# Moving eight PSUM copies of the kv sums from ScalarE to VectorE

## Chip, cores and metric

One core of one Trainium2 chip. The metric is device time in microseconds (us); lower is better. Engines are named as in the profile: PE is TensorE's matmuls, PEld its weight loads, DVE VectorE, ACT ScalarE, POOL GpSimd, SP the engine that issues most DMAs. "L614" is line 614 of the kernel.

## The reference, cut to what matters

```python
S, D, H, Dh = 2048, 1024, 32, 32
q, k, v = split(x @ wqkv)                      # 32 heads of 32
phi_q = [softmax(q w_phi), softmax(-q w_phi)]  # 64 features per head
phi_k = [softmax(k w_phi), softmax(-k w_phi)]
kv  = einsum("bhsf,bhsd->bhfd", phi_k, v)      # summed over the whole sequence
z   = einsum("bhsf->bhf", phi_k)
num = einsum("bhqf,bhfd->bhqd", phi_q, kv)
o   = num / (einsum("bhqf,bhf->bhq", phi_q, z) + 1e-6)
a   = o @ wo
b   = x, with a gated FFN added to the one row that a router picks
out = g * a + (1 - g) * b                      # g = sigmoid(x . gate_w), per row
```

The kv sums need every row of the sequence, so the kernel has two halves: the k side builds kv in PSUM, the memory in which the kernel puts the results of its matmuls, then kv is copied in bf16 to SBUF, from where the matmuls of the q side read it. The change is in the copy between the two halves.

## The kernel before

The program goes through a scheduler that orders each engine's instructions. The parts that matter, cuts marked with "...":

```python
psA = ...tile_pool(name="psA", bufs=2, space=PSUM)   # pq tiles: two buffers
psK = ...tile_pool(name="psK", bufs=1, space=PSUM)   # kvps, later num: ONE buffer
kvps = psK.tile([P, 3 * 512], F32, name="kvps", tag="kvn")

def kv_finish(ops, copy):                            # L606
    kvr = kvps[:, 0:16 * KSTR].rearrange("p (j half c) -> p j half c", half=2, c=KSTR)
    for op in ops:
        jh, half, hh_, sg = op // 8, op // 4 % 2, op // 2 % 2, op % 2
        ...
        copy(out=KV[jh][h4 * 32:h4 * 32 + 32, sg, :, h4 * 33:h4 * 33 + 33],     # L614
             in_=kvr[q * 32:q * 32 + 32, js, half, hh_ * 33:hh_ * 33 + 33])

def q_front(sb, j):
    pq = psA.tile([P, SB], F32, name="pq", tag="pA")
    for kb in range(KB):                             # 8 matmuls: "a pq group"
        nc.tensor.matmul(pq[:], ...)                                            # L627
    nc.scalar.activation(out=E[:, j, 0, :], in_=pq[:], func=ACTF.Exp)           # L629
    nc.scalar.activation(out=E[:, j, 1, :], in_=pq[:], func=ACTF.Exp, scale=-1.0)  # L630

def q_num(t, hf):
    num = psK.tile([P, 3 * 512], F32, name="num", tag="kvn")
    ... 8 matmuls num <- E, KV[hf]                                              # L648
    nc.vector.reciprocal(out=rS, in_=nb[:, :, 132:136])                         # L657 (rq)
    ... T <- num * rS on VectorE                                                # L662

    kv_finish(range(8), nc.vector.tensor_copy)       # into KV[0]
    kv_finish(range(8, 16), nc.scalar.copy)          # into KV[1]
    ...
    while i < n_front + NL + 2 or wq_:               # the q side
        ... q_num of step i - 7 ...
        if NPRE <= i < n_front:
            q_front(i // KB, i % KB)
        ... q_wo: 8 matmuls "po" (L705), result to HBM
```

A pq group needs one of two PSUM buffers, which the second exponential of an earlier group frees. The first num needs the one buffer that kvps holds until the last of the 16 copies; in the trace of the kernel before it is recorded as waiting 0.98 us for them. The whole kernel:

Of the kernel before, what the change touches and what calls it, by code (L numbers as in the profile page):

```python
# [167 lines left out]
def kernel(  # L168
# [4 lines left out]
    nc = tc.nc  # L173
# [433 lines left out]
# [4 lines that stand above are left out]
            js = slice(jh * 4, jh * 4 + 4)  # L611
            h4 = half * 2 + hh_
            q = hh_ * 2 + sg
            copy(out=KV[jh][h4 * 32:h4 * 32 + 32, sg, :, h4 * 33:h4 * 33 + 33],  # L614
                 in_=kvr[q * 32:q * 32 + 32, js, half, hh_ * 33:hh_ * 33 + 33])
# [167 lines left out]
            one_hot_sums()  # L783
    qp["eb"] = None
    kv_finish(range(8), nc.vector.tensor_copy)
    kv_finish(range(8, 16), nc.scalar.copy)
    kscope.close()
    qp["eb"] = main.enter_context(tc.tile_pool(name="eb", bufs=1))
    qp["qw"] = main.enter_context(tc.tile_pool(name="qw", bufs=2))
# [77 lines left out]
```

## Time and profile before

| kernel before | |
|---|---|
| device time, median of 3 (range) | 280.58 us (280.07 to 280.60) |
| span of the profiled run | 279.5 us (a fourth run, 281.24 us long) |
| TensorE busy | 271.8 us, 97% |
| VectorE / ScalarE / GpSimd busy | 67% / 44% / 50% |
| the 16 copies (L614) | 8 on VectorE, median 292 ns; 8 on ScalarE, median 264 ns |

A timeline line has start, length, engine, line, operation, output<-input, count, and in brackets how long the engine was idle before it and what released it. "Pitch" is the time from one start to the next in a row of like instructions; small_ps are small matmuls of the FFN row, which the scheduler puts between the others. A line of the windows table has the stretch, its length, the busy us (and instructions) of PE, PEld, DVE, ACT and POOL, then the granted TensorE clock, the DMA share and GB/s. The engine that matters is TensorE, so what counts is where it stops. The lines are in the prediction.

### The profile page before, as it was taken

To read this page: it belongs to the slowest core of one execution; us is meant where nothing else is said; L and a number is where in the kernel's file an instruction comes from. 1 tells how busy PE (TensorE), PEld (TensorE's weight loads), DVE (VectorE), ACT (ScalarE), POOL (GpSimd) and SP (SyncE) were. 2 spreads that over 40 slices of the span, in tenths; PEclk is the share of its full clock that TensorE was granted. 3 is DMA by queue.
4 is the path that set the end of the run, shared out by engine and by line. 5 is a ranking of instruction groups with operands and counts; after the bars stand their busy time and mean duration, and the time that the engine had idled before them with its cause. 6 is when DMAs were issued, how large, how long until landed. Compare 5 with 4: busy or idle time off the path is not lost.

```text
span 279.5 us, 5440 instructions
## 1 busy us (share of the span) xinstructions
PE 271.8 (97%) x2022; PEld 149.7 (54%) x2022; DVE 186.2 (67%) x386; ACT 121.9 (44%) x235; POOL 140.9 (50%) x152
## 2 busy tenths in 40 slices
PE   7999999999999999999999899999999999999994
PEld 3666667676544455455554354554555555555442
DVE  3020025566799898699993287888766677899862
ACT  3143332232455546454564657855445543323300
POOL 8000000000087989847862078999566555798310
PEclk9999999999999999999999999999999999999999
DMA  7899993854963788985705817843897244425631
GB/s 257 215 177 187 161 179 76 133 107 130 394 258 114 276 311 298 353 295 189 281 0 188 302 49 260 201 99 13 28 174 202 68 94 125 129 96 133 150 98 62
DMA packets 68767, 47.97 MB, mean 172 GB/s; under 512 B 51376, under 2 KB 56576, under 8 KB 68736
## 3 DMA queue, kind: packets, MB, share of 16 engines
q1 hardware_dynamic: 68240, 47.10, 63.4%
q10 hardware_dynamic: 464, 0.48, 0.5%
q8 instruction: 17, 0.28, 0.4%
q14 instruction: 14, 0.11, 0.1%
q0 software_dynamic: 32, 0.00, 0.0%
HBM read 31.00 MB, written 4.20 MB: 126 GB/s over the span
## 4 chain that ended last, share of the span: by engine, by line
PE 83%; DMA 7%; DVE 4%; issue 2%; ACT 2%; POOL 2%; DVEq 0%; POOLq 0%
PE po L705 20%; PE pq L627 19%; PE pv L536 17%; PE pk L578 11%; PE num L648 6%; DMA wch<-in_B_w_up_dram 3%; DMA mrow<-mi 3%; PE pW L313 2%; PE kvps L602 2%; DVE ssum L586 2%; PE facc L475 1%; PE pv L558 1%; DMA xs_t<-in_A_x_dram 1%; PE kvps L558 1%; PE small_ps L490 1%
## 5 line engine op out<-in xcount | busy, mean ns | idle before, releaser
L578 PE MATMUL pk<-wkf,xT 128*128 128x512 bf16 x256 | 60.4, 379 | 0.0
L627 PE MATMUL pq<-xT,wqf 128*128 128x512 bf16 x256 | 60.2, 379 | 0.0
L677 POOL TENSOR_TENSOR U<-T 128x512 f32<-128x512 f32 x32 | 41.5, 1298 | 34.2 <-DVE T L662 16.7
L705 PE MATMUL po<-wo_sb,oT 128*128 128x512 bf16 (+2 forms) x264 | 58.6, 373 | 0.0
L536 PE MATMUL pv<-wv_sb,xT 128*128 128x256 bf16 (+2 forms) x336 | 52.9, 307 | 0.0
L593 POOL TENSOR_TENSOR phi<-e,rs 128x1024 bf16<-128x1024 bf16 x24 | 45.8, 1912 | 4.0 <-DVE cnd L343 2.4
L586 DVE TENSOR_REDUCE ssum<-e 128x32 f32<-128x1024 bf16 x32 | 38.1, 1194 | 3.8 <-ACT e L582 3.3
L705 PEld LDWEIGHTS <-oT 128*128 128x128 bf16 x264 | 25.4, 98 | 27.8
L536 PEld LDWEIGHTS <-xT 128*128 128x128 bf16 x336 | 31.4, 97 | 14.7
L662 DVE TENSOR_TENSOR T<-num,rq 128x1024 f32<-128x1024 f32 x32 | 38.9, 1215 | 0.0
L543 ACT CAST v_all<-pv 128x384 bf16<-128x384 f32 (+1 forms) x45 | 20.1, 447 | 41.8 <-PE pv L536 36.0
L627 PEld LDWEIGHTS <-wqf 128*128 128x128 bf16 x256 | 23.8, 98 | 24.1 <-issue 0.6
L708 DVE SCALAR_TENSOR_TENSOR o_out<-po,gate,xg 128x512 bf16<-128x512 f32 (+2 forms) x33 | 23.9, 729 | 18.4 <-PE po L705 17.2
L578 PEld LDWEIGHTS <-xT 128*128 128x128 bf16 x256 | 23.0, 97 | 22.8
L678 POOL TENSOR_TENSOR o_sb<-U,rden 128x512 bf16<-128x512 f32 x32 | 33.6, 1049 | 2.5
L581 ACT ACTIVATE e<-pk 128x512 bf16<-128x512 f32 x32 | 19.1, 597 | 32.3 <-PE pk L578 21.9
L629 ACT ACTIVATE E<-pq 128x512 bf16<-128x512 f32 x32 | 19.0, 595 | 30.5 <-PE pq L627 30.2
L423 POOL COPY wch<-wT 1x1 bf16<-1x1 bf16 x3 | 0.4, 177 | 58.6 <-DMA wT<-in_A_wqkv_dram 58.6
L590 POOL TENSOR_TENSOR ksum<-ksum,ssum 128x32 f32<-128x32 f32 x32 | 13.0, 405 | 20.7 <-DVE ssum L586 15.3
L648 PEld LDWEIGHTS <-E 128*128 128x128 bf16 x256 | 16.4, 98 | 10.5 <-DVE T L662 5.2
L648 PE MATMUL num<-KV,E 128*128 128x136 bf16 x256 | 20.7, 223 | 1.0 <-ACT KV L614 1.0
L630 ACT ACTIVATE E<-pq 128x512 bf16<-128x512 f32 x32 | 18.9, 591 | 0.0
(140 smaller groups left out, 253.7 us busy)
## 6 DMA issues: line engine op xcount, KB each, us to landing
wchd<-in_B_w_down_dram SPq DMA_DIRECT2D x7, 1024.0 KB
wch<-in_B_w_up_dram SPq DMA_DIRECT2D x6, 1024.0 KB
wch<-in_B_w_gate_dram SPq DMA_DIRECT2D x4, 1024.0 KB
xin<-in_A_x_dram SPq DMA_DIRECT2D x16, 256.0 KB
out_dram<-o_out SPq DMA_DIRECT2D x30, 128.0 KB
wch<-in_B_w_gate_dram SPq DMA_DIRECT2D x4, 768.0 KB
wv_sb<-in_A_wqkv_dram SPq DMA_DIRECT2D x8, 256.0 KB
wo_sb<-in_A_wo_dram SPq DMA_DIRECT2D x1, 2048.0 KB
```

What stands on the lines that cost most here:

```text
L536: nc.tensor.matmul(pv[:, 0:hi - lo], lhsT=xT[:, kb, t * P:(t + 1) * P], rhs=wv_sb[:, kb, lo:hi], start=(kb == 0), stop=(kb == KB - 1))
L543: nc.scalar.copy(out=v_all[:, t, h0:h1, 0:DH], in_=pv[:, 0:(h1 - h0) * DH].rearrange("p (h d) -> p h d", d=DH))
L578: nc.tensor.matmul(pkf, lhsT=xT[:, kb, t * P:(t + 1) * P], rhs=wkf[:, kb, hf * 512:(hf + 1) * 512], start=(kb == 0), stop=(kb == KB - 1))
L586: nc.vector.tensor_reduce(out=ssum[:], in_=e2, axis=AX.X, op=ALU.add)
L593: eng.tensor_tensor(out=phi[:].rearrange("p h s f -> p (h s) f"), in0=e2, in1=_bc(rs[:], [P, HH * 2, DH]), op=ALU.mult)
L627: nc.tensor.matmul(pq[:], lhsT=wqf[:, kb, j * P:(j + 1) * P], rhs=xT[:, kb, sb * SB:(sb + 1) * SB], start=(kb == 0), stop=(kb == KB - 1))
L648: nc.tensor.matmul(num[:, b * NSTR:b * NSTR + KVW], lhsT=E[:, j, sg, tl * P:(tl + 1) * P], rhs=KV[hf][:, sg, jl, :], start=True, stop=True)
L662: nc.vector.tensor_tensor(out=T[:].rearrange("p s (j h) d -> p (s j) h d", h=4), in0=nv[:, :, :, 0:DH], in1=rS.unsqueeze(3).to_broadcast([ ...
L677: nc.gpsimd.tensor_tensor(out=U[:], in0=T[:, 0], in1=T[:, 1], op=ALU.add)
L678: nc.gpsimd.tensor_tensor(out=st["o"][:, hf * HH:(hf + 1) * HH, :], in0=U[:], in1=_bc(rden[:], [P, HH, DH]), op=ALU.mult)
L705: nc.tensor.matmul(po[:, 0:w], lhsT=st["oT"][:, kb, :], rhs=wo_sb[:, kb, sl], start=(kb == 0), stop=(kb == KB - 1))
L708: nc.vector.scalar_tensor_tensor(out=o_out[:, 0:w], in0=po[:, 0:w], scalar=gate[:, t:t + 1], in1=st["xg"][:, sl], op0=ALU.mult, op1=ALU.add)
```

## The change

Its intent: all copies of the kv sums on VectorE, which is idle there (4.88 us, from its own eight copies to rq); ScalarE is relieved.

```diff
     kv_finish(range(8), nc.vector.tensor_copy)
-    kv_finish(range(8, 16), nc.scalar.copy)
+    kv_finish(range(8, 16), nc.vector.tensor_copy)
     kscope.close()
```

## The prediction

> **What bounds the kernel now.** I read the page of the kernel before first: busy times, then the chain that ended last.
>
> ```profile
> span 279.5 us, 5440 instructions
> PE 271.8 (97%) x2022; PEld 149.7 (54%) x2022; DVE 186.2 (67%) x386; ACT 121.9 (44%) x235; POOL 140.9 (50%) x152
> PE 83%; DMA 7%; DVE 4%; issue 2%; ACT 2%; POOL 2%; DVEq 0%; POOLq 0%
> ```
>
> TensorE is busy 97% of the span and 83% of the chain is its work. The other engines matter only where TensorE stops for them. The change touches 16 small copies of the kv sums out of PSUM (line 614), so I asked next for the waits of that line's neighbourhood, 152.7 to 162.1 us (engine, line, what it waited for, us in total, times, longest):
>
> ```profile
> DVE rq L657 <- PE num L648: 4.9, 1, 4.9
> DVE KV L614 <- PE kvps L602: 2.9, 1, 2.9
> PE num L648 <- ACT KV L614: 1.0, 1, 1.0
> ACT KV L614 <- DVE KV L614: 0.2, 1, 0.2
> ```
>
> TensorE waits once, 1.0 us, for ScalarE's copies; ScalarE's copies wait for VectorE's, although they fill another tile; VectorE then has 4.9 us of nothing to do. The timeline of the same stretch (start, length, engine, line, operation, count) shows the order:
>
> ```profile
> 152.72 3.61 PE L627 MATMUL pq<-xT,wqf 128*128 128x512 bf16 x16
> 152.91 2.44 DVE L614 CAST KV<-kvps 32x132 bf16<-32x132 f32 x8 [2.93 <-PE kvps L602]
> 154.64 0.60 ACT L629 ACTIVATE E<-pq 128x512 bf16<-128x512 f32 x1 [1.15 <-PE pq L627]
> 155.39 2.19 ACT L614 CAST KV<-kvps 32x132 bf16<-32x132 f32 x8 [0.15 <-DVE KV L614]
> 156.26 0.39 PE L490 MATMUL small_ps<-wchd,hh 128*32 128x512 bf16 x1
> 157.60 0.60 ACT L630 ACTIVATE E<-pq 128x512 bf16<-128x512 f32 x1
> 157.63 0.57 PE L648 MATMUL num<-KV,E 128*128 128x136 bf16 x7 [0.98 <-ACT KV L614]
> 158.25 1.89 PE L627 MATMUL pq<-xT,wqf 128*128 128x512 bf16 x8
> 160.03 2.11 PE L627 MATMUL pq<-xT,wqf 128*128 128x512 bf16 x9
> 160.23 0.36 DVE L657 RECIPROCAL rq<-num 128x32 f32<-128x32 f32 x1 [4.88 <-PE num L648]
> 162.00 0.65 PE L648 MATMUL num<-KV,E 128*128 128x136 bf16 x8
> ```
>
> The copies are one chain of 16: VectorE's eight from 152.91, then ScalarE's eight from 155.39 to 157.58. The first num needs all 16, because it takes the PSUM buffer that the copies empty (pool psK has one). ScalarE's eight copies also stand in its program ahead of the second exponential (L630) of the pq group done at about 154.5. Pool psA has two buffers, so this exponential, held back to 157.60, gates the pq group that starts at 158.25. Thus both things that TensorE could do, num and the next pq, hang on ScalarE's copies.
>
> [...] ScalarE idles 0.15 us and starts at 155.39, just after VectorE's last copy at about 155.36. So the split over two engines never ran in parallel, and moving the second half gives up no overlap.
> [...] The trace has medians of 292 and 264 ns; I use the trace.
> [...]
>
> **The change part by part.** It removes eight copies from ScalarE (2.19 us) and adds eight on VectorE, directly behind the eight that are there. The order of the instructions of the changed kernel, engine by engine, shows that the scheduler also rearranged TensorE: behind the two pq groups (16 matmuls) there now follows a third pq group of eight, then all eight num matmuls of the first step. Before, one small_ps matmul and seven num came first, then the third pq, then the eighth num. From the fourth pq on, the order is the same up to the small_ps block, which takes the postponed matmul (24 instead of 23). On ScalarE the two exponentials stand next to each other.
>
> Copies: the pitch on VectorE is 2.44/8 = 0.305 us. Sixteen end at 152.91 + 16 x 0.305 = 157.79, against 157.58 before: 0.2 us later. VectorE was idle until 160.23, so these 2.4 us of work displace nothing.
>
> Exponential: it follows L629 at 154.64 at the 0.49 us pitch of such pairs (157.60 to 158.09) and ends at 155.13 + 0.60 = 155.73. The third pq finds its buffer free.
>
> TensorE: the pitch of a 512-column matmul is (3.61 - 0.38)/15 = 0.215 us. The 16 pq are issued by 152.72 + 3.44 = 156.16. The third pq goes on at once, to 156.16 + 1.72 = 157.88. There the copies have been done for 0.1 us, so num starts at 157.88 to 157.9. Eight num have a pitch of 0.061 us, 0.49 in all, last end 0.65 after the first start.
>
> The next mark is the second num, at 162.00 before. It needs the fourth pq and one more matmul, 9 x 0.215 = 1.94: TensorE is ready at 157.9 + 0.49 + 1.94 = 160.33. It also needs VectorE to have emptied the first num. Before, this took from rq at 160.23 to 162.00 = 1.77; now rq can start at 157.9 + 0.65 + 0.04 = 158.59 and the buffer is free at 160.36. So the second num moves from 162.00 to 160.36: 1.64 us. One small_ps matmul is only postponed, at its pitch in the later block (1.41/23 = 0.06 us). Net 1.58 us.
>
> As a cross-check by removal: from 156.16 to 162.00 are 5.84 us, and the work in it is 0.06 + 17 x 0.215 + 8 x 0.061 = 4.21. The idle pitch time is 1.63 us, larger than the 0.98 of the waits view because that counts from the modelled end of the last matmul (0.39 long, pitch 0.06), and because of 0.2 us for the late exponential and 0.1 us before small_ps. After the change hardly any of it is left.
>
> Does it reach the end? Everything behind is tight and relative. In the chain in order of time every piece from 158.25 to 275.45 is TensorE, and the table by windows (us, TensorE busy) shows no hole:
>
> ```profile
> 152.70:160.20 7.50, 6.48 (x40) 3.05 (x37) 2.35 (x8) 5.10 (x15) 0.00 (x0) 1.00 0.88 315
> 160.20:170.00 9.80, 9.80 (x80) 4.67 (x79) 8.11 (x20) 5.40 (x10) 7.45 (x8) 1.00 0.35 115
> 180.00:200.00 20.00, 20.00 (x137) 10.41 (x135) 15.69 (x39) 10.61 (x21) 17.99 (x18) 1.00 0.56 64
> 240.00:260.00 20.00, 20.00 (x129) 10.40 (x128) 19.61 (x46) 5.37 (x8) 16.29 (x14) 1.00 0.42 115
> ```
>
> The loads behind (wo, 2 MB, at 164.9; the transposes) are triggered by work that moves along, and wo is first used at 190. The tail after 275.45 stays. So 280.58 - 1.58 = 279.0 us.
>
> **The rivals.**
> (a) The copies stay the gate, and are now slower: 16 x 0.305 instead of 8 x 0.305 + 8 x 0.273, so num starts 0.2 us later: 280.8. For it: num waited for exactly this chain. Against: in the new order 1.72 us of pq stand ahead of num, and fill just the time that the copies take. The margin is only 0.1 us; a wait that is missed by 0.1 costs 0.1.
> (b) Only the 0.98 us that the waits view names comes back[...]: 279.6. Against: pitches are what a dense stream is counted in, and elsewhere it is dense.
> (c) The gain is given back: the num loop of 160 to 190 is paced by VectorE and TensorE alike (2.46 us a step, VectorE busy 8.11 of 9.80). For a loss: a load may not come earlier with it. rq waits in the program for eight DMA semaphores, and the row loads (xin) and w_down chunks run until about 160 (DMA share 0.88 in the window above). If one of these is what rq really waits for, rq stays near 160.2 and the result is 280.4. Against: the DMA waits are program waits of VectorE's queue that passed in 50 ns each at 153.8 to 154.2, and rq's buffer replaces tiles that were loaded long before. The first pass of the loop starts earlier on both engines, so its pace is no objection.
>
> **Range and chances.** The mechanism (idle TensorE filled) I give 80%, with 1.3 to 1.8 us; (b) 10%; (c) or (a) 10%. Runs of the kernel before spread by 0.5 us. So 279.0, range 278.4 to 280.1. A gain of 2% would need 5.6 us, more than three times the idle time there; a loss of 2% has no source. Chances 0.01, 0.98, 0.01.
>
> **What would show it right or wrong.** Right: 16 VectorE copies from about 152.9 to 157.8; no ScalarE copy; L630 at about 155.1; 24 pq matmuls in one run from 152.7; num at about 157.9 with little or no wait on VectorE's KV; second num at about 160.4; 24 small_ps near 167; last po about 1.6 us earlier. Wrong: a TensorE wait for DVE KV of several tenths (a); rq started clearly later than num's end, released by a DMA (c); a new TensorE gap between 160 and 275, or a second num at 160.4 with an end that has not moved.

The forecast's sum is 280.58 - 1.58 = 279.0 us, and its terms are figures of the trace. The 292 and 264 ns are the copies' medians on VectorE and ScalarE.

## The result and the profile after

279.25 us (four runs, 278.64 to 279.72) against 280.59 us (280.07 to 280.70). The ratio is 0.9955, 95% interval 0.993 to 0.9979. A ratio is the mean time of one kernel's runs over that of the other's runs of the same rounds, so not quite the ratio of the quoted medians. Faster by half a per cent, well within 2%, as predicted.

The head of the page after, and its chain that ended last:

```profile
span 277.4 us, 5439 instructions
PE 270.7 (98%) x2022; PEld 149.8 (54%) x2022; DVE 188.0 (68%) x394; ACT 119.6 (43%) x227; POOL 141.1 (51%) x152
PE 94%; DMA 4%; ACT 0%; DVE 0%; issue 0%
```

The timeline after, the stretch that answers to that of before:

```profile
151.85 5.34 PE L627 MATMUL pq<-xT,wqf 128*128 128x512 bf16 x24
152.05 4.89 DVE L614 CAST KV<-kvps 32x132 bf16<-32x132 f32 x16 [2.92 <-PE kvps L602]
...
154.27 0.59 ACT L630 ACTIVATE E<-pq 128x512 bf16<-128x512 f32 x1
...
157.00 0.49 PEld L648 LDWEIGHTS <-E 128*128 128x128 bf16 x8 [0.30 <-DVE KV L614]
157.03 0.64 PE L648 MATMUL num<-KV,E 128*128 128x136 bf16 x8
...
157.50 2.11 PE L627 MATMUL pq<-xT,wqf 128*128 128x512 bf16 x9
157.70 0.36 DVE L657 RECIPROCAL rq<-num 128x32 f32<-128x32 f32 x1 [0.76 <-PE num L648]
...
159.48 0.65 PE L648 MATMUL num<-KV,E 128*128 128x136 bf16 x8
```

And the waits of that stretch (152.7 to 162.1 us):

```profile
DVE rq L657 <- PE num L648: 1.1, 2, 0.8
PEld L648 <- DVE T L662: 0.7, 2, 0.4
PEld L648 <- DVE KV L614: 0.3, 1, 0.3
```

What to see: 24 pq matmuls run without a hole where there were 16, a 0.98 us stop, seven num and another stop. The second exponential (L630) runs directly behind the first, not 2.96 us behind it. The num matmuls carry no wait in brackets; only a weight load was held 0.30 us by the last copy, and this wait ran beside the matmuls: the load started at 157.00, and the pq matmuls are recorded until 151.85 + 5.34 = 157.19. VectorE's idle time ahead of rq fell from 4.88 to 0.76 us.

**Marks for comparing traces.** The spans differ by 2.1 us, more than the median times do; the profiled runs were ones of 281.24 and 279.04 us. To separate the change from what differs between executions I use three marks in each trace: A, the start of the pq run behind the last kvps matmul; B, the start of the second num group; C, the start of the last run of 64 po matmuls.

| trace | A | B - A | C - A | span - C |
|---|---|---|---|---|
| before | 152.72 | 9.28 | 110.42 | 16.36 |
| after | 151.85 | 7.63 | 108.77 | 16.78 |
| difference | -0.87 | -1.65 | -1.65 | +0.42 |

Between A and B the kernel gained 1.65 us, and from B to C nothing of that was lost. The 0.87 us ahead of A and the 0.42 us in the tail need another explanation, since the traces show the same order of instructions on every engine there; that is experiment 1's and 5's question.

### The profile page after: what moved, and what is told of

Same layout as the page of the kernel before. It is cut to its first block, busy times and chain, and to the rows that moved or that the text cites. A ratio compares the mean times of both kernels' runs of the same rounds, so it can differ in the third digit from the quotient of the medians.

```text
span 277.4 us, 5439 instructions
## 1 busy us (share of the span) xinstructions
PE 270.7 (98%) x2022; PEld 149.8 (54%) x2022; DVE 188.0 (68%) x394; ACT 119.6 (43%) x227; POOL 141.1 (51%) x152
## 4 chain that ended last, share of the span: by engine, by line
PE 94%; DMA 4%; ACT 0%; DVE 0%; issue 0%
PE pq L627 20%; PE po L705 20%; PE pk L578 18%; PE pv L536 18%; PE num L648 6%; DMA wch<-in_B_w_up_dram 3%; PE pW L313 3%; PE kvps L602 3%; PE facc L475 2%; DMA xs_t<-in_A_x_dram 1%; PE pv L558 1%; PE kvps L558 1%; PE small_ps L490 1%; PE pT L294 1%; ACT xT L295 0%; DVE o_out L708 0%
## 5 line engine op out<-in xcount | busy, mean ns | idle before, releaser
L581 ACT ACTIVATE e<-pk 128x512 bf16<-128x512 f32 x32 | 19.1, 597 | 31.3 <-PE pk L578 22.8
L629 ACT ACTIVATE E<-pq 128x512 bf16<-128x512 f32 x32 | 19.0, 594 | 31.2 <-PE pq L627 30.9
L582 ACT ACTIVATE e<-pk 128x512 bf16<-128x512 f32 x32 | 18.9, 591 | 0.0
```

## The experiments

All ran on one chip, number 15 in the record, which doesn't name that of the first comparison; the kernel before took 281.06 us there (median of 12 runs, 280.43 to 282.67). All results were correct, and all runs in the fast state but experiment 5, whose single run has no state. A run-to-run spread of up to 2.2 us against effects of 0.5 to 2 us means that the marks in the traces decide, and the times only confirm.

### 1 and 5. Both kernels again

No edit. What was expected of the changed kernel, and then of the kernel before:

> The changed kernel again, unaltered, for a second trace and a tighter ratio. Marks in the trace: A = start of the pq run that follows the last kvps matmul, B = start of the second num group, C = start of the last run of 64 po. Before: A 152.72, B - A = 9.28, C - A = 110.42. First trace of the change: A 151.85, B - A = 7.63, C - A = 108.77. Theory (the change acts only between A and B): B - A again 7.6 to 7.7 and C - A about 108.8, while A scatters by some tenths up to a microsecond between executions, whichever the kernel, because its orders up to A are the same. Time ratio to before 0.994 to 0.996. Rival (the change also makes A earlier, so the gain is 2.1 us as the first two spans suggest): A again near 151.9, ratio 0.9925.

> The kernel before, unaltered, for a second trace. In the five traces of changed kernels A (start of the pq run behind the last kvps matmul) is 151.6 to 152.1 us and the tail from the start of the last 64 po to the end is 16.8 to 16.9; in the one trace of before they are 152.72 and 16.36. Theory (the change acts between A and B only; up to A the orders on all engines are the same): B - A = 9.3 and C - A = 110.4 again, while A falls among the others', 151.6 to 152.7, and the tail is 16.4 to 16.9. Rival (something of the change acts before A or in the tail): A near 152.7 and tail near 16.4 again.

Measured: after, 278.99 us (6 runs), ratio 0.9925 (0.9901 to 0.9949), A 152.11, B - A 7.62, C - A 108.75, tail 16.94. Before, one run of 281.05 us, A 152.01, B - A 9.29, C - A 110.41, tail 16.88. Its timeline repeats the first trace's stop to the hundredth:

```profile
155.56 0.39 PE L490 MATMUL small_ps<-wchd,hh 128*32 128x512 bf16 x1
156.92 0.57 PE L648 MATMUL num<-KV,E 128*128 128x136 bf16 x7 [0.98 <-ACT KV L614]
157.54 1.89 PE L627 MATMUL pq<-xT,wqf 128*128 128x512 bf16 x8
```

The ratio, 0.9925, is the very figure of the rival; it is the marks that speak against it. B - A and C - A repeat within 0.02 us in either kernel. A does not belong to a kernel: 152.72 and 152.01 before, 151.85 and 152.11 after. The tail of before is 16.36 and 16.88, that of after 16.78 and 16.94. So the rivals fall: as far as two traces of each can show, the change acts between A and B only. In the first trace of before the chain shows a piece that is not in the chains of the others, a small DMA round trip of the router's row, 7.22 us long, ahead of A:

```profile
70.08 7.22 DMA mrow<-mi
```

Its first user started at 77.3 us there, and at 75.8 to 76.5 us in the nine other traces. That this alone moved A was not tested. The change is worth 1.65/280.6 = 0.59%, a ratio of 0.9941, which lies inside both measured intervals; the two intervals (around 0.9955 and 0.9925) overlap.

### 2. The old split, with ScalarE's copies behind the exponential

```diff
     kv_finish(range(8), nc.vector.tensor_copy)
-    kv_finish(range(8, 16), nc.scalar.copy)
 ...
             q_front(i // KB, i % KB)
+            if i == NPRE:
+                kv_finish(range(8, 16), nc.scalar.copy)
```

> The split of before (8 copies VectorE, 8 ScalarE), but ScalarE's eight are written behind the pq group whose second exponential they held back. The build puts that exponential ahead of them, and TensorE's order becomes that of the changed kernel. Theory (the gain is the exponential set free, which lets TensorE do the third pq while the copies run; which engine copies does not matter): copies end about A + 5.2, num at A + 5.2 to 5.3, B - A = 7.7, time as the changed kernel within 0.1 us: ratio to before about 0.995. Rival 1 (VectorE as such, or one engine less in the chain of copies, makes the gain): B - A near 9.3, ratio 1.000. Rival 2 (both parts matter): half way, 8.5.

Measured: 279.61 us, ratio 0.9944 (0.9917 to 0.997), A 152.09. num at A + 5.18, just as in the changed kernel, but B - A 8.16, between the theory's 7.7 and the rival's half way. C - A 109.28: of the 1.65 us, 1.14 came without any copy on VectorE beyond the first eight. The timeline shows where the other 0.5 went:

```profile
154.51 0.59 ACT L630 ACTIVATE E<-pq 128x512 bf16<-128x512 f32 x1
154.99 2.17 ACT L614 CAST KV<-kvps 32x132 bf16<-32x132 f32 x8
157.18 0.60 ACT L629 ACTIVATE E<-pq 128x512 bf16<-128x512 f32 x1
...
157.27 0.64 PE L648 MATMUL num<-KV,E 128*128 128x136 bf16 x8
...
158.31 2.10 PE L627 MATMUL pq<-xT,wqf 128*128 128x512 bf16 x9 [0.41 <-ACT E L630]
```

My expectation missed this. With the first group's exponentials ahead of the copies, it is the second group's that queue behind them (157.18), and the fourth pq waits 0.41 us for its buffer. So one part of the theory stands, the exponential set free is most of the gain, and the part "which engine copies does not matter" falls: in every place on ScalarE that was tried (before, here, and in experiments 3 and 8) the copies delay some exponential; in the latter three TensorE has a recorded wait for one, 0.41, 0.38 and 0.53 us.

### 3. The engines exchanged

```diff
-    kv_finish(range(8), nc.vector.tensor_copy)
-    kv_finish(range(8, 16), nc.scalar.copy)
+    kv_finish(range(8), nc.scalar.copy)
+    kv_finish(range(8, 16), nc.vector.tensor_copy)
```

> The split with the engines exchanged: ScalarE copies the first eight, VectorE the second eight. ScalarE's copies can start only after the exponential that runs at A (about A + 0.8), end about A + 3.0, and the two exponentials of the first pq group of the run follow, ended at about A + 4.05. Theory (the freed pq buffer paces TensorE): the third pq starts at A + 4.1 instead of A + 3.44, num at A + 5.8, B - A = 8.3; of the gain of 1.65 us 0.65 is lost, ratio to before about 0.9975. Rival (only the end of the 16 copies counts): that end is at about A + 5.45, so num at A + 5.5 and B - A = 8.0 or less.

Measured: 279.37 us, ratio 0.9956 (0.9926 to 0.9987), A 151.64. Third pq at A + 4.00 (expected 4.1), num at A + 5.72 (5.8), B - A 8.17 (8.3), C - A 109.29.

```profile
152.30 2.17 ACT L614 CAST KV<-kvps 32x132 bf16<-32x132 f32 x8
...
154.51 2.44 DVE L614 CAST KV<-kvps 32x132 bf16<-32x132 f32 x8 [5.61 <-ACT KV L614]
155.00 0.59 ACT L630 ACTIVATE E<-pq 128x512 bf16<-128x512 f32 x1
...
155.64 1.89 PE L627 MATMUL pq<-xT,wqf 128*128 128x512 bf16 x8 [0.38 <-ACT E L630]
...
157.36 0.64 PE L648 MATMUL num<-KV,E 128*128 128x136 bf16 x8
```

The last copy ended at 154.51 + 2.44 = 156.95, 0.41 us ahead of num, so the end of the copies was not the limit; the third pq was, and that waited for L630. The rival falls. Note also that now VectorE's copies wait for ScalarE's: ScalarE's last ended at 152.30 + 2.17 = 154.47, VectorE's first started at 154.51. In both orders the engine that comes second waited.

### 4. ScalarE's load put back, first try

```diff
+    scr = const.tile([P, 4, 33], BF, name="scr")
+    for _ in range(8):
+        nc.scalar.copy(out=scr[0:32], in_=KV[0][0:32, 0, :, 0:33])
```

(added to the changed kernel behind its copies)

> The changed kernel (16 copies on VectorE) with ScalarE's lost load put back as eight useless copies of the finished first half into a scratch tile, at the place where its eight copies stood. The build puts six of them ahead of the second exponential of the first pq group. The result stays right. Theory (ScalarE's delay of the exponentials costs the time): fillers of 0.27 to 0.35 us from A + 2.65, exponential ends A + 5.5 to 6.0, third pq starts A + 5.6 to 6.1, TensorE idles 2.2 to 2.6 us there, B - A = 9.8 to 10.2, ratio to before about 1.002. Rival (having all copies on VectorE is what gains): B - A stays near 7.7, ratio 0.995.

Measured: 279.16 us, ratio 0.9942 (0.9914 to 0.9971), A 151.56, B - A 7.66, C - A 108.79, the rival's numbers. But the experiment did not do what it was meant to. The useless copies read a part of KV that the first VectorE copy alone had written, so five of them ran from 152.22 to 153.83, in the idle time of ScalarE ahead of the exponential, and L630 still ended at 155.00, A + 3.44, when the third pq wants it. It says nothing for the rival and shows only that ScalarE work in that idle time is free. Experiment 6 is the mended one.

### 6. The exponential delayed, all copies on VectorE

```diff
     nc.scalar.activation(out=E[:, j, 0, :], in_=pq[:], func=ACTF.Exp)
+    if sb == 0 and j == NPRE:
+        for c in range(3):
+            nc.scalar.copy(out=E[:, j, 1, :], in_=E[:, j, 0, :])
     nc.scalar.activation(out=E[:, j, 1, :], in_=pq[:], func=ACTF.Exp, scale=-1.0)
```

> The changed kernel with three useless ScalarE copies between the two exponentials of the first pq group of the run (they write the place that the second exponential then overwrites, so the result is right). All kv copies stay on VectorE. The build moves one copy and both exponentials of the next group ahead of the second exponential, and fills TensorE with 16 small_ps matmuls from the later block. Theory (the late exponential is what costs): second exponential ends at about A + 6.1, third pq starts at about A + 6.1 to 6.2; work between A and there is 3.44 + 16 x 0.061 + 0.49 = 4.9, so 1.2 to 1.3 us idle and C - A = 110.0 (changed kernel 108.77, before 110.42); ratio to before 0.996 to 0.999. Rival (VectorE's taking all copies is the gain): C - A stays 108.8.

Measured: 280.65 us, ratio 0.9982 (0.9951 to 1.0013), A 152.16, C - A 110.21 (expected 110.0; changed kernel 108.77). In its timeline the lines behind 629 are shifted by three: L633 is the second exponential, L651 num.

```profile
152.16 3.61 PE L627 MATMUL pq<-xT,wqf 128*128 128x512 bf16 x16
152.36 4.89 DVE L614 CAST KV<-kvps 32x132 bf16<-32x132 f32 x16 [2.94 <-PE kvps L602]
...
156.88 1.08 ACT L633 ACTIVATE E<-pq 128x512 bf16<-128x512 f32 x2
...
157.31 0.65 PE L651 MATMUL num<-KV,E 128*128 128x136 bf16 x8 [0.78 <-DVE KV L614]
...
157.88 0.61 PE L490 MATMUL small_ps<-wchd,hh 128*32 128x512 bf16 x7
...
158.43 3.63 PE L627 MATMUL pq<-xT,wqf 128*128 128x512 bf16 x16
```

VectorE's copies are those of the changed kernel, 4.89 us long, and yet 1.44 of the 1.65 us are gone (110.21 - 108.77), because L633 of the first group, the second of the two, ended at 157.96 = A + 5.8 and the third pq started at A + 6.27, behind what the build put there to fill. The stop that the trace records is not at the third pq but at num: 0.78 us for the last copy, which ended at A + 5.09 as in the changed kernel. There the third pq ran in this time; here the build had put it behind num, and it could not have run in this time anyway, its buffer being free only at A + 5.8. This is the converse of experiment 2: delaying the exponential, with the order that the build then chooses, undoes nearly all of the gain.

### 7. Twenty copies in place of sixteen

```diff
     kv_finish(range(8, 16), nc.vector.tensor_copy)
+    kv_finish(range(8, 8 + 4), nc.vector.tensor_copy)
```

> The changed kernel with four of the copies done twice, 20 in one VectorE chain instead of 16. The build puts one matmul of the fourth pq ahead of num; the exponentials are untouched. Theory (the chain of copies has hardly any slack against the three pq groups): copies end at A + 0.2 + 16 x 0.305 + 4 x 0.31 to 0.36 = A + 6.3 to 6.5, TensorE is ready for num at A + 5.17 + 0.22 = A + 5.4, so 0.9 to 1.1 us idle and C - A = 109.7 to 109.9, ratio to before 0.995 to 0.998. Rival (the copies are hidden and longer ones would be too): num at A + 5.4, C - A 108.8.

Measured: 280.67 us, ratio 0.9989 (0.9958 to 1.002), A 151.49, C - A 109.88 (expected 109.7 to 109.9), num at A + 6.51.

```profile
151.49 5.56 PE L627 MATMUL pq<-xT,wqf 128*128 128x512 bf16 x25
151.68 6.26 DVE L614 CAST KV<-kvps 32x132 bf16<-32x132 f32 x20 [2.94 <-PE kvps L602]
...
158.00 0.65 PE L648 MATMUL num<-KV,E 128*128 128x136 bf16 x8 [0.96 <-DVE KV L614]
```

The first rival of the prediction (a) exists, then, but behind a limit that 16 copies just do not reach: four more, 1.37 us, cost 1.11 us (109.88 - 108.77). Of the difference, 0.26 us, 0.22 are the one pq matmul that the build moved ahead of num: num itself moved from A + 5.18 to A + 6.51, by 1.33 of the 1.37 us. So the slack of the 16 copies was about 0.04 us. The time ratio is worse than the marks say, since this trace's tail was the longest of all, 17.53 us.

### 8. All copies on ScalarE

```diff
-    kv_finish(range(8), nc.vector.tensor_copy)
+    kv_finish(range(8), nc.scalar.copy)
     kv_finish(range(8, 16), nc.scalar.copy)
```

> All 16 copies on ScalarE, none on VectorE: the mirror of the change. They start behind the exponential that runs at A, at about A + 0.75, at 0.273 each, and end at A + 5.1; the two exponentials of the first pq group follow and end at A + 6.2. TensorE's order is that of before without the small_ps matmul (seven num, third pq, eighth num). Theory (exponentials held back pace TensorE): num at A + 5.2, third pq at A + 6.25, B - A = 6.25 + 1.72 + 0.06 + 1.94 = 10.0, C - A about 111.1 to 111.2, ratio to before 1.002 to 1.003. Rival (one chain on one engine is what gains, whichever the engine; its copies are also the shorter ones): B - A 7.7, ratio 0.995.

Measured: 281.22 us, ratio 1.0022 (0.9985 to 1.0059), A 151.92, B - A 9.93 (expected 10.0), C - A 111.08 (111.1 to 111.2), tail 16.30.

```profile
152.58 4.36 ACT L614 CAST KV<-kvps 32x132 bf16<-32x132 f32 x16
156.96 0.60 ACT L629 ACTIVATE E<-pq 128x512 bf16<-128x512 f32 x1
156.99 0.57 PE L648 MATMUL num<-KV,E 128*128 128x136 bf16 x7 [1.45 <-ACT KV L614]
...
158.10 1.89 PE L627 MATMUL pq<-xT,wqf 128*128 128x512 bf16 x8 [0.53 <-ACT E L630]
```

The copies end at A + 5.02, earlier than the 5.09 of the changed kernel, and it is the slowest of all by its marks. So neither one chain on one engine nor an early end of it is the gain; both exponentials behind the chain are the loss.

What no run varied is the order of TensorE's instructions by itself: the build sets it from the program. In the kernel before it could not have been the cause alone, for the exponential that frees the third pq's buffer ended at 157.60 + 0.60 = 158.20, after the stop that this pq would have had to fill had ended (157.63).

No version beat the changed kernel by its marks, and none was to be expected there: 24 pq matmuls at 5.34 us are (5.34 - 0.38)/23 = 0.216 us each, the pitch of the dense stretches, so between A and num nothing is left to fill.

## Why the prediction was right, point by point

**The copies end 0.2 us later, and it does not matter: right.** Predicted end A + 5.07, measured 152.05 + 4.89 = 156.94, A + 5.09. Experiment 7 shows that the margin was even thinner than the 0.1 us said, about 0.04.

**The exponential ends at A + 3.01 and frees the third pq: right.** Measured 154.27 + 0.59 = 154.86, A + 3.01. That this is what pays is shown from both sides: experiment 2 frees it and gets 1.14 us, experiment 6 delays it and loses 1.44 us.

**First num at A + 5.16 to 5.18, second at A + 7.64: right.** Measured A + 5.18 and A + 7.63. The gain there, predicted 1.64, is 1.65 us.

**One small_ps matmul only postponed, 0.06 us to pay: wrong, by that much.** The later block of 24 lasted as long as that of 23, 1.41 us between its first matmul and the next num (166.05 to 167.46 after, 168.57 to 169.98 before). In both, the weight load of that num was held 0.42 us until VectorE's rden (L669), so TensorE was not the limit there and the postponed matmul is hidden. So 1.65, not 1.58 us, reaches C.

**Everything reaches the end: right for C, unclear in the time by scatter.** The medians differ by 1.34 us in the first comparison and by 2.07 us in the second; A and the tail scatter by about 1.2 us each over the ten traces.

**Rival (a)**, the copies as a new gate: refuted for 16 copies, shown for 20. **Rival (b)**, only the 0.98 us of the waits view: refuted, 1.65 us came back. The view starts the wait where the last matmul's recorded 0.39 us end, and the other parts of the idle time have no entry of this size. **Rival (c)**, rq waiting for a DMA: refuted, rq started at 157.70, 0.03 us after the last num matmul's end at 157.67.

**Why the copies did not run in parallel before: not shown.** Experiment 3 has the same wait the other way round (VectorE's first copy at 154.51, ScalarE's last ended at 154.47), so in both orders the second engine waited. The wait is in the program: in the packed trace the last VectorE copy (155.05) raises semaphore 100, and the first ScalarE copy (155.39) waits for it. By the source that last copy (op 7) reads partitions 96 to 127 and the first of ScalarE (op 8) partitions 0 to 31. Why the build lets the whole half finish first stays open, and no run took the wait out. The gain doesn't rest on it.

## What to carry to other kernels

Before giving an engine small work, ask what stands behind it in its queue: here eight copies of 0.27 us cost TensorE 1.65 us because an exponential that frees a PSUM buffer stood behind them (the first exponential of the same pq group ran at 154.64, this one at 157.60, directly after the copies), while the same copies were free, with about 0.04 us to spare, on an engine with nothing urgent to do. Splitting copies of one PSUM tile over two engines bought no overlap in these traces (the second engine began 0.03 us behind the first one's last copy, 0.04 us in experiment 3), because the program made the second engine wait, so here the question of which engine to use was one of queues, not of speed: ScalarE's copies were the shorter ones, 264 against 292 ns. And compare traces by marks around the change: the spans said 2.1 us, the times 1.3 and 2.1 us, the marks 1.65 and 1.66 us.
